# Row maxima of an attention round in one instruction instead of two, with other margins in the planner that lists the kernel's instructions

## The chip, the cores and the metric

The kernel runs on one core of a Trainium2 chip. The metric is the device time of one execution in microseconds (us); of several executions the median is given. Five engines work side by side, each through its own list of instructions in order: PE (TensorE, matrix products), DVE (VectorE), ACT (ScalarE), POOL (GpSimd) and SP (SyncE, which here only issues DMA transfers). Semaphores hold an instruction back until what it needs is there. PE writes to PSUM, a small memory of eight banks; everything else lies in SBUF or in the chip's main memory.

## The reference

The work is an attention over 8 batches and 8 heads of 576 tokens with 64 dimensions, which leaves out every score that is more than tau under the maximum of its row, and then an MLP mixer over tokens (576 to 256 to 576) and channels (512 to 1536 to 512). All is float32.

```python
scores = scale * np.matmul(q, k.transpose(0, 1, 3, 2))
thresh = np.max(scores, axis=-1, keepdims=True) - tau
scores = np.where(scores >= thresh, scores, -1000000000.0)
attn = np.exp(scores - np.max(scores, axis=-1, keepdims=True))
attn = attn / (np.sum(attn, axis=-1, keepdims=True) + 1e-09)
x = np.matmul(attn, v)          # then (B,H,S,D) -> (B, S, H*D)
h = np.maximum(x.transpose(0, 2, 1) @ w_tok1, 0.0) @ w_tok2
u = x + h.transpose(0, 2, 1)
out = u + np.maximum(u @ w_ch1, 0.0) @ w_ch2
```

## The kernel before, in words

**Tiles and stages.** Attention is cut into 144 units: 128 query rows (two heads of one batch side by side) against all 576 keys, 18 units to a batch. Two units make a round, 72 rounds in all, nine to a batch ("row" in the code). A round goes through all engines:

- PE forms the scores of both units and both heads (`scores_of_two`, line 1000) in the tile `sc`, which takes five of the eight banks. There is one such tile, so the next round's scores can't begin before the masks of this round have read it. The two heads lie at the two ends of the tile (`AT`, line 959): head 0 of both units in columns 0 to 1152, head 1 in columns 1408 to 2560. Both touch the third bank.
- DVE takes the maximum of each row (`top`, line 1025): one instruction for head 0 of both units and one for head 1, 1152 elements for each partition.
- POOL turns the maxima into the bias of the threshold (`shift`, line 1031), again one instruction for each head, of two elements for each partition.
- ACT applies the mask (`mask`, line 1043), four instructions of 576 elements, and the exponential with its sum (`exps`, line 1053), four more. Each of these is followed by a short read of the sum. The masks read `sc`; when all four are done, `sc` is free.
- DVE inverts the sums (lines 309 and 310), POOL scales the weights (`scale`, line 318), DVE transposes them in blocks (`T`, line 346), SP moves the blocks to their places (`eT`, line 356), and PE multiplies them with the values (line 404). In the first batch PE transposes instead (line 333, copied out in line 338) and the values are line 388.

The mixer's products are mixed in between: the token products of a batch (lines 485, 522, 535, 553) and its channel products (lines 1243, 1167, 1258). For each batch only a part of the channel products is done during attention. The rest is spilled to main memory and done after the last round, in a long stage of products by Strassen's scheme (line 1663). In the first 110 us the weights are also unpacked from a wide form on ACT, DVE and POOL (lines 228 to 252), and PE is given transposes that nobody reads (`keep_warm`, line 775) where it would stand still.

**Who sets the order.** When the program is built, a planner (`Scheduler`, lines 662 to 830) holds a clock for each engine and a list of operations with a cost in us, an engine, a rank and what they depend on. It always lists next the operation that can start first by its clocks, and of those that can start at once the one with the lower rank. The list is fixed from then on; on the chip each engine runs through its list and waits where something is late. What the planner counts therefore decides which work stands ahead of which, and nothing else. An operation may start at the end of what it depends on, plus that operation's `lag` (0.2 unless given) when it comes from another engine.

In a round (`make_round`, lines 1411 to 1465) the planner counts `SCORES` for the scores, 1.27 for each maximum, 0.24 for each shift, 0.64 for each mask with a lag of 0.25, 0.77 for each exponential. The loop over the masks goes over the heads outside and the units inside. A mask depends on the shift and the maximum of its head; those of the odd unit depend on the maximum of head 1 as well.

**The margins that the change touches.**

- `SLACK` and `SPARE` (line 636; `sure`, lines 698 to 702): an operation of PE that could start at once stands behind others if what it depends on ended less than `SLACK` ago on another engine, or landed less than `SPARE` ago.
- `NEAR`, `KEEP` and `KEEP_LAST` (lines 637, 730, 1059, 1496): scores are held until the mixer's products done so far reach a planned amount, less `KEEP` (for the last row `KEEP_LAST`), and less `NEAR` right behind values.
- `FLIGHT`, `RATE`, `LANDING` (lines 638, 707, 753 to 760): the planner's picture of the transfers: so many in flight at once, so many KB for each us, so long to land.
- `LATE` and `LATE_PE` (lines 705 and 706): once PE's clock is past `CALM`, an operation of DVE or PE that needs a transfer is planned this much after the landing.
- `WARM_GAP` and `WARM_TURN` (line 770): how many warm-up transposes are put into a gap of PE in the first 110 us.
- `SCORES` (line 1058): cost of a score block.

Of the kernel before, what the change touches and what calls it, by code (L numbers as in the profile page):

```python
# [14 lines left out]
ALU = mybir.AluOpType  # L15
AX = mybir.AxisListType
# [5 lines left out]
def kernel(  # L22
# [25 lines left out]
    nc = tc.nc  # L48
    B, H, S, D = q.shape
# [18 lines left out]
    SCALE = 1.0 / 8.0  # L68
# [192 lines left out]
    toff = const.tile([P, 1], F32, name="toff")  # L261
# [44 lines left out]
    def inverse(us):  # L306
        rs = sums_of[us[0] // 2 % RS]
        rr = small.tile([P, 2, 2], F32, tag="rr", name=f"rr_{us[0]}")
        nc.vector.tensor_reduce(out=rr, in_=rs, axis=AX.X, op=ALU.add)
        nc.vector.reciprocal(out=rr, in_=rr)  # L310
        for i, u in enumerate(us):
            st[u] = st[u][0], rr[:, i]

    def scale(u):
        e, rr = st[u]
        for h in range(2):
            eh = half(u, e, h)
            nc.gpsimd.tensor_scalar(out=eh, in0=eh, scalar1=rr[:, h : h + 1], scalar2=1.0, op0=ALU.mult, op1=ALU.mult)  # L318
        st[u] = e
# [23 lines left out]
    def turn_blocks(u):  # L343

        T = Ts[u] = att.tile([P, 4, NK * 32], F32, tag="T", bufs=3, name=f"T_{u}")
        nc.vector.transpose(out=T, in_=st.pop(u).rearrange("p a c x -> p a (c x)"))  # L346
# [286 lines left out]
        nc.vector.tensor_scalar(out=ntau, in0=toff, scalar1=SCALE, scalar2=None, op0=ALU.mult)  # L633

    TOKEN_RANK, TOKEN_AFTER_TOKEN = 1.5, 2.5
    SLACK, SPARE = 0.8, 3.5
    NEAR = 8
    FLIGHT, RATE, LANDING, LATE, LATE_PE, CALM = 12, 205.0, 1.5, 1.0, 0.0, 200.0
    WARM_UNTIL, WARM_GAP, WARM_TURN = 110.0, 0.6, 0.11

    class Op:

# [15 lines left out]
    class Scheduler:  # L658
# [59 lines left out]
        def pick(self, eng):  # L718
# [3 lines left out]
            for x in self.ready[eng]:  # L722
# [6 lines left out]
                c = t if t > now + 0.02 else now, eng == "pe" and self.sure(x) > now + 0.02, rank, x.index  # L729
                if x.rank == 1 and eng == "pe" and self.done < x.plan - (NEAR if self.after_values else 0.0):  # L730
                    held = c, t, x
# [109 lines left out]
    sched = Scheduler()  # L841
# [3 lines left out]
    def key_op(*key):  # L845
        return keyed.get(key)

    def put(key, x):
        keyed[key] = x
        return x  # L850
# [45 lines left out]
    def rank_of_group(b, p0, g):  # L896
        return ((b * NP + p0) // 2) * 3 + g
# [61 lines left out]
    AT = (0, 5 * MAIN - 2 * S)  # L959
# [60 lines left out]
            st[u] = [sc[:, at + S * k : at + S * k + S] for at in AT], bias[:, :, k : k + 1]  # L1020

    tops = {}
    def top(it, h):
        sc, mx, _ = tops[it]
        nc.vector.tensor_reduce(  # L1025
            out=mx[:, h], in_=sc[:, AT[h] : AT[h] + 2 * S].rearrange("p (k x) -> p k x", k=2), axis=AX.X, op=ALU.max
        )

    def shift(it, h):
        _, mx, bias = tops[it]  # L1030
        nc.gpsimd.tensor_scalar(out=bias[:, h], in0=mx[:, h], scalar1=toff, scalar2=-SCALE, op0=ALU.add, op1=ALU.mult)  # L1031

    def mask(u, h):
        if h == 0:
            part, bias = st[u]
            rs = sums_of[u // 2 % RS][:, u % 2]
            e = home_of(u)
            masked[u] = e, rs, part, bias
        e, rs, part, bias = masked[u]
        scores = part[h]  # L1040
        if in_blocks(units[u][0]):
            scores = scores.rearrange("p (a c y) -> p a c y", a=4, c=NK)
        nc.scalar.activation(out=half(u, e, h), in_=scores, func=AF.Prelu, bias=bias[:, h], scale=SCALE, alpha=STEEP)  # L1043
        if h == 1:
            del masked[u]
            st[u] = e, rs
# [3 lines left out]
    def exps(u, h):  # L1050
        e, rs = st[u] if u not in masked else masked[u][0:2]
        eh = half(u, e, h)
        nc.scalar.activation(out=eh, in_=eh, func=AF.Exp, bias=ntau, accum_out=rs[:, h, 0:1])  # L1053
# [1 line left out]

    UNITS = len(units)
    ROUNDS = UNITS // 2
    SCORES, VALUES, VALUES_IN_HALVES = 2.2, 3.45, 3.3
    KEEP, KEEP_LAST = 22.5, 25.5


    fills = {}
# [348 lines left out]
    def make_round(it):  # L1411
        us = (2 * it, 2 * it + 1)
        pre = [key_op("pre", u - 2, h) for u in us for h in range(2)]
        prepared = []
        for u in us:
            b, p0, t = units[u]
            n = b * NP + p0
            for m in [n] * (t <= SHARED) + [n + 1] * (t >= SHARED):
                prepared += [key_op("prep", m, 0) if it else None, key_op("prep", m, 1)]
                prepared += [key_op("prep", 0, "first")] if not it else []  # L1420
        x = put(("S", it), sched.op("pe", SCORES, lambda: scores_of_two(us, keyed["S", it].mark_eng), pre + prepared, 1 if it >= UB // 2 else -1))
        urgent = -1 if it < UB // 2 else 0
        row, k = divmod(it, UB // 2)
        x.plan = planned_at(row - 1, k) if row else -1.0
        x.scores = True
        for h in range(2):
            put(("mx", it, h), sched.op("dve", 1.27, lambda h=h: top(it, h), (x,), urgent))
            put(("bias", it, h), sched.op("pool", 0.24, lambda h=h: shift(it, h), (key_op("mx", it, h),), urgent))
        for h in range(2):
            for u in us:  # L1430
                deps = [key_op("bias", it, h), key_op("mx", it, h)]
                if h == 0:
                    deps += [key_op("T", u - 4), key_op("pre", u - 1, 0)]
                else:
                    deps.append(key_op("pre", u, 0))
                if u % 2:
                    deps.append(key_op("mx", it, 1))
                put(("pre", u, h), sched.op("act", 0.64, lambda u=u, h=h: mask(u, h), deps, urgent or 1, lag=0.25))
        for u in us:
            for h in range(2):  # L1440
                put(("exp", u, h), sched.op("act", 0.77, lambda u=u, h=h: exps(u, h), (key_op("pre", u, h),), 2, lag=0.3))
        n = sched.op("dve", 0.38, lambda: inverse(us), [key_op("exp", u, h) for u in us for h in range(2)], 2)
        for u in us:
            b, p0, t = units[u]
            s = sched.op("pool", 1.46, lambda u=u: scale(u), (n,), 1)
            deps = [s]
            G = rank_of_group(b, p0, t // GU)
            opens, closes = [u == end(where[b, p0, t - t % GU + i] for i in range(GU)) for end in (min, max)]
            if not b:
                deps += [key_op("V", G - 2) if opens else None, key_op("T", u - 1)]  # L1450
                for third in range(3):
                    x, y = sched.banked(
                        0.33,
                        lambda bank, u=u, third=third: turn(u, third, bank),
                        "act",
                        0.4,
                        lambda bank, u=u, third=third: turned(u, third, bank, nc.scalar.copy),
                        deps,
                        0,
                        other=("dve", 0.5, lambda bank, u=u, third=third: turned(u, third, bank, nc.vector.tensor_copy)),  # L1460
                    )
                    put(("turned", u, third), y)
                    deps = [x]
                put(("T", u), x)
                if closes:
                    make_group(b, p0, t // GU)
                    if t // GU == 2 and p0:
                        rows_due.append(b)
                continue
            deps += [key_op("T", u - 1), key_op("M", u - 3)]  # L1470
            put(("T", u), sched.op("dve", 1.31, lambda u=u: turn_blocks(u), deps, 4))
            put(
                ("M", u),
                sched.op(
                    "sp",
                    2.4,
                    lambda u=u: move(u),
                    (key_op("T", u), key_op("V", G - 2) if opens else None),
                    0,
                    after=(key_op("M", u - 1),),  # L1480
                    dmas=(4, 147, 0.69),
                ),
            )
            if closes:
                make_group(b, p0, t // GU)
                if t // GU == 2:
                    (rows_due if p0 == NP - 2 else early_due).append(b)
# [3 lines left out]
    def planned_at(row, k):  # L1491

        work = [TOKENS - SAVED * (r > 0) + NOW[r] * SEVEN + (GROUP - SEVEN) * (not r) for r in range(B - 1)] + [0.0]
        total = sum(work[:row])
        part = work[row]
        return total + part * (k - 2) / (UB // 2) - (KEEP_LAST if row == B - 2 else KEEP)
# [529 lines left out]
```

## Time and profile before

| what | us |
|---|---|
| median of 3 runs (1209.57 to 1210.18) | 1209.9 |
| the profiled execution | 1203.62 |
| its span, first to last instruction | 1201.8 |
| PE busy in 0 to 110 us / 110 to 793 / 793 to 1202 | 101.90 / 666.30 / 404.12 |
| of it warm-up transposes up to 110 us | 30.75 |
| DVE, ACT and POOL busy in the span | 881.9, 608.9, 336.6 |
| first and last maximum of a round start at | 8.6 and 789.2 |
| one maximum (1152 elements), one shift (2 elements) | 1.344, 0.276 |
| one mask, one exponential (576 elements) | 0.742, 0.784 |

The profile was taken by the hardware in one execution. An instruction's line in it is a line of the kernel. A group's row has its busy time, the mean duration of one in ns, and, behind the bar, how long the engine stood idle ahead of them and which engine's instruction ended that. A wait is put down to the instruction that came last. PE's busy time is modelled from the starts, so it is no measure of how close PE is to its peak. In the timeline a row has the start in us, the duration from the first to the last instruction of a merged group, the engine, the line, what is written and read, how many instructions it merges, and in brackets the idle time ahead.

### The profile page before, as it was taken

Reading aid. Unit: us, or ns where it says so; the run is one execution under the profiler, and the core shown is the slowest. Engines: PE = TensorE matmul, PEld = TensorE weight load, DVE = VectorE, ACT = ScalarE, POOL = GpSimd, SP = SyncE. Lnnn points to the kernel's source line nnn. Section 1 sums busy time; section 2 is a strip of 40 time slices with the busy share of each in tenths; the row PEclk is TensorE's granted clock in tenths of the full one; section 3 lists DMA queues with packets and bytes.
Section 4 is the critical chain, followed back from the end, with each engine's and each line's share of the span. In section 5 each row is a group of like instructions: output and inputs, shape, how many; then the busy total and the mean of one; then the engine's idle time right before and its main releaser. Section 6 shows DMA issues by size and latency. Waiting matters only on the chain.

```text
span 1201.8 us, 29350 instructions
## 1 busy us (share of the span) xinstructions
PE 1172.3 (98%) x11526; PEld 979.0 (81%) x11526; DVE 881.9 (73%) x1504; ACT 608.9 (51%) x1392; POOL 336.6 (28%) x577
## 2 busy tenths in 40 slices
PE   8999999999989999999999999999999999999998
PEld 7666878877768768877887887888899999999988
DVE  6788987678578668757866866854778687786866
ACT  6999775555664566555555556541231413223230
POOL 3576553244235324423433423421100000000000
PEclk9999999999999999999999999999999999999999
DMA  7655877678778778777877877671210302122020
GB/s 151 146 138 151 213 193 196 148 164 209 171 163 196 174 177 190 186 166 192 198 171 178 196 187 163 177 186 43 92 36 10 84 15 71 36 51 56 12 60 36
DMA packets 302154, 161.73 MB, mean 135 GB/s; under 512 B 191744, under 2 KB 287040, under 8 KB 301888
## 3 DMA queue, kind: packets, MB, share of 16 engines
q1 hardware_dynamic: 299856, 159.11, 54.9%
q8 instruction: 91, 1.49, 0.5%
q10 hardware_dynamic: 2160, 0.74, 0.2%
q14 instruction: 47, 0.39, 0.1%
HBM read 56.75 MB, written 14.68 MB: 59 GB/s over the span
## 4 chain that ended last, share of the span: by engine, by line
PE 69%; ACT 9%; DVE 7%; SPq 6%; DMA 5%; issue 2%; POOL 2%; DVEq 0%; ACTq 0%; POOLq 0%
PE bank L1663 29%; PE bank L1167 10%; PE bank L1243 8%; PE sc L1000 8%; PE bank L404 7%; ACT e L1043 4%; DVE mx L1025 4%; ACT e L1053 3%; SPq L356 3%; DMA eT<-T 2%; PE bank L553 2%; SPq L119 2%; PE bank L1258 2%; POOL e L318 2%; PE bank L522 1%
## 5 line engine op out<-in xcount | busy, mean ns | idle before, releaser
L1043 ACT ACTIVATE e<-sc,bias 128x576 f32<-128x576 f32 x288 | 194.3, 742 | 205.4 <-DVE mx L1025 102.0
L318 POOL TENSOR_SCALAR e<-e,rr 128x576 f32<-128x576 f32 x288 | 216.3, 771 | 128.9 <-DVE rr L310 106.5
L1053 ACT ACTIVATE e<-e,ntau 128x576 f32<-128x576 f32 x288 | 221.5, 784 | 0.6
L1025 DVE TENSOR_REDUCE mx<-sc 128x2 f32<-128x1152 f32 x144 | 187.6, 1344 | 34.7 <-PE sc L1000 34.6
L346 DVE STREAM_TRANSPOSE T<-e 128x1152 f32<-128x1152 f32 x126 | 170.0, 1360 | 16.9 <-POOL e L318 15.0
L1243 PE MATMUL bank<-xT,wc 128*128 128x256 f32 x768 | 175.1, 383 | 0.0
L1000 PE MATMUL sc<-kT,qT 64*64 64x384 f32 (+2 forms) x3456 | 159.6, 327 | 10.1 <-ACT e L1043 10.0
L1243 PEld LDWEIGHTS bank<-xT,wc 128*128 128x128 f32 x768 | 143.2, 190 | 25.1 <-issue 4.6
L1000 PEld LDWEIGHTS sc<-kT,qT 64*64 64x64 f32 x3456 | 101.3, 133 | 69.0 <-issue 46.2
L404 PE MATMUL bank<-eT,lv 64*64 64x192 f32 x3024 | 136.4, 325 | 7.8 <-DMA eT<-T 5.9
L404 PEld LDWEIGHTS bank<-eT,lv 64*64 64x64 f32 x3024 | 115.0, 133 | 26.9 <-issue 6.1
L1778 ACT COPY temps<-bank 128x256 f32<-128x256 f32 x90 | 33.4, 371 | 90.2 <-PE bank L1663 90.2
L1167 PE MATMUL bank<-wc,g 128*128 128x256 f32 x336 | 76.3, 379 | 0.0
L1167 PEld LDWEIGHTS bank<-wc,g 128*128 128x128 f32 x336 | 63.6, 190 | 8.7
L553 PE MATMUL bank<-w,a 128*128 128x192 f32 (+1 forms) x256 | 67.0, 412 | 0.0
L968 POOL MEMSET mark_pool<- 128x1 f32 x57 | 5.8, 103 | 207.3 <-PE sc L1000 178.9
L1031 POOL TENSOR_SCALAR bias<-mx,toff 128x2 f32<-128x2 f32 x144 | 39.2, 276 | 81.4 <-DVE mx L1025 79.2
L1663 PE MATMUL bank<-t,w1s 128*128 128x256 f32 x240 | 60.6, 379 | 0.0
L1167 PE MATMUL bank<-w2s,g 128*128 128x256 f32 x252 | 59.9, 387 | 0.7 <-DVE g L1131 0.7
L1053 ACT ACTIVATION_READ_ACCUMULATOR e<-e,ntau 128x1 f32 x288 | 59.9, 208 | 0.0
L1663 PE MATMUL bank<-t,wc 128*128 128x256 f32 x240 | 59.3, 379 | 0.0
L1663 PE MATMUL bank<-u,wc 128*128 128x256 f32 x240 | 58.5, 379 | 0.0
(196 smaller groups left out, 1834.2 us busy)
## 6 DMA issues: line engine op xcount, KB each, us to landing
eT<-T SPq DMA_DIRECT2D x504, 144.0 KB, 3.0
lv<-in_v_dram SPq DMA_DIRECT2D x112, 144.0 KB, 3.0
w2s<-in_moe_w_ch_dram SPq DMA_DIRECT2D x24, 512.0 KB, 3.9
lk<-in_k_dram SPq DMA_DIRECT2D x122, 72.0 KB, 3.0
ut<-us SPq DMA_DIRECT2D x136, 64.0 KB, 2.1
lq<-in_q_dram SPq DMA_DIRECT2D x120, 72.0 KB, 2.9
out_dram<-us SPq DMA_DIRECT2D x30, 256.0 KB, 2.7
u<-spill SPq DMA_DIRECT2D x8, 512.0 KB, 4.5
```

The lines of the kernel that those rows point to most:

```text
L318: nc.gpsimd.tensor_scalar(out=eh, in0=eh, scalar1=rr[:, h : h + 1], scalar2=1.0, op0=ALU.mult, op1=ALU.mult)
L346: nc.vector.transpose(out=T, in_=st.pop(u).rearrange("p a c x -> p a (c x)"))
L404: nc.tensor.matmul(to[o], lhsT=lv[half][r, c, :], rhs=eT[r, M * half : M * half + M, c, :], start=c == 0, stop=c == NK - 1, skip_group_che ...
L553: nc.tensor.matmul(bank[:, n * i : n * i + n], lhsT=hidden[b][:, m, P * c : P * c + P], rhs=w2[:, m, lo : lo + n], start=(m == 0), stop=(m ...
L1000: x = nc.tensor.matmul(sc[rows, at + lo : at + hi], lhsT=qT[r, cols], rhs=kT[r, lo:hi], start=True, stop=True, skip_group_check=True,)
L1025: nc.vector.tensor_reduce(out=mx[:, h], in_=sc[:, AT[h] : AT[h] + 2 * S].rearrange("p (k x) -> p k x", k=2), axis=AX.X, op=ALU.max)
L1031: nc.gpsimd.tensor_scalar(out=bias[:, h], in0=mx[:, h], scalar1=toff, scalar2=-SCALE, op0=ALU.add, op1=ALU.mult)
L1043: nc.scalar.activation(out=half(u, e, h), in_=scores, func=AF.Prelu, bias=bias[:, h], scale=SCALE, alpha=STEEP)
L1053: nc.scalar.activation(out=eh, in_=eh, func=AF.Exp, bias=ntau, accum_out=rs[:, h, 0:1])
L1167: nc.tensor.matmul(bank[:, 0:HD], lhsT=x[:, j, :], rhs=y[:, j, :], start=j == 0, stop=j == HJ - 1)
L1243: nc.tensor.matmul(bank[:, 0:n], lhsT=wc1[:, j, c, :], rhs=uT[:, c, GR * i : GR * i + n], start=(c == 0), stop=(c == NCC - 1))
L1663: nc.tensor.matmul(to, lhsT=l, rhs=r, start=start and x == 0, stop=x == len(pairs) - 1, skip_group_check=not start)
```

## The change

The two maxima of a round become one instruction that reads both ends of the score tile, and the two shifts become one. In the planner the round has one maximum of 2.53 us and one shift of 0.25, all four masks depend on these, and the odd unit's extra dependence goes. Ten of the planner's numbers change: `SLACK`, `SPARE`, `NEAR`, `FLIGHT`, `RATE`, `LATE_PE`, `WARM_GAP`, `SCORES`, `KEEP` and `KEEP_LAST`. What is computed stays the same.

```diff
@@ -633,10 +633,10 @@
         nc.vector.tensor_scalar(out=ntau, in0=toff, scalar1=SCALE, scalar2=None, op0=ALU.mult)
 
     TOKEN_RANK, TOKEN_AFTER_TOKEN = 1.5, 2.5
-    SLACK, SPARE = 0.8, 3.5
-    NEAR = 8
-    FLIGHT, RATE, LANDING, LATE, LATE_PE, CALM = 12, 205.0, 1.5, 1.0, 0.0, 200.0
-    WARM_UNTIL, WARM_GAP, WARM_TURN = 110.0, 0.6, 0.11
+    SLACK, SPARE = 1.0, 4.5
+    NEAR = 12.0
+    FLIGHT, RATE, LANDING, LATE, LATE_PE, CALM = 8, 214.0, 1.5, 1.0, 1.0, 200.0
+    WARM_UNTIL, WARM_GAP, WARM_TURN = 110.0, 0.4, 0.11
 
     class Op:
 
@@ -1020,15 +1020,14 @@
             st[u] = [sc[:, at + S * k : at + S * k + S] for at in AT], bias[:, :, k : k + 1]
 
     tops = {}
-    def top(it, h):
+    def top(it):
         sc, mx, _ = tops[it]
-        nc.vector.tensor_reduce(
-            out=mx[:, h], in_=sc[:, AT[h] : AT[h] + 2 * S].rearrange("p (k x) -> p k x", k=2), axis=AX.X, op=ALU.max
-        )
-
-    def shift(it, h):
+        both = bass.AP(tensor=sc.tensor, offset=sc.offset, ap=[sc.ap[0], [AT[1], 2], [S, 2], [1, S]])
+        nc.vector.tensor_reduce(out=mx, in_=both, axis=AX.X, op=ALU.max)
+
+    def shift(it):
         _, mx, bias = tops[it]
-        nc.gpsimd.tensor_scalar(out=bias[:, h], in0=mx[:, h], scalar1=toff, scalar2=-SCALE, op0=ALU.add, op1=ALU.mult)
+        nc.gpsimd.tensor_scalar(out=bias, in0=mx, scalar1=toff, scalar2=-SCALE, op0=ALU.add, op1=ALU.mult)
 
     def mask(u, h):
         if h == 0:
@@ -1055,8 +1054,8 @@
 
     UNITS = len(units)
     ROUNDS = UNITS // 2
-    SCORES, VALUES, VALUES_IN_HALVES = 2.2, 3.45, 3.3
-    KEEP, KEEP_LAST = 22.5, 25.5
+    SCORES, VALUES, VALUES_IN_HALVES = 2.4, 3.45, 3.3
+    KEEP, KEEP_LAST = 26.0, 27.0
 
 
     fills = {}
@@ -1423,18 +1422,15 @@
         row, k = divmod(it, UB // 2)
         x.plan = planned_at(row - 1, k) if row else -1.0
         x.scores = True
-        for h in range(2):
-            put(("mx", it, h), sched.op("dve", 1.27, lambda h=h: top(it, h), (x,), urgent))
-            put(("bias", it, h), sched.op("pool", 0.24, lambda h=h: shift(it, h), (key_op("mx", it, h),), urgent))
+        put(("mx", it), sched.op("dve", 2.53, lambda: top(it), (x,), urgent))
+        put(("bias", it), sched.op("pool", 0.25, lambda: shift(it), (key_op("mx", it),), urgent))
         for h in range(2):
             for u in us:
-                deps = [key_op("bias", it, h), key_op("mx", it, h)]
+                deps = [key_op("bias", it), key_op("mx", it)]
                 if h == 0:
                     deps += [key_op("T", u - 4), key_op("pre", u - 1, 0)]
                 else:
                     deps.append(key_op("pre", u, 0))
-                if u % 2:
-                    deps.append(key_op("mx", it, 1))
                 put(("pre", u, h), sched.op("act", 0.64, lambda u=u, h=h: mask(u, h), deps, urgent or 1, lag=0.25))
         for u in us:
             for h in range(2):
```

## The prediction

> **What bounds the kernel now.** I read the page first, then busy time by stage, then the waits of PE between 160 and 793 us, then the timeline of single rounds.
>
> ```profile
> PE 1172.3 (98%) x11526; PEld 979.0 (81%) x11526; DVE 881.9 (73%) x1504; ACT 608.9 (51%) x1392; POOL 336.6 (28%) x577
> PE 69%; ACT 9%; DVE 7%; SPq 6%; DMA 5%; issue 2%; POOL 2%; DVEq 0%; ACTq 0%; POOLq 0%
> 0.00:110.00 110.00, 101.90 (x1118) 76.74 (x1118) 85.43 (x154) 93.80 (x197) 63.42 (x105) 1.00 0.63 143
> 110.00:793.00 683.00, 666.30 (x7773) 531.84 (x7774) 504.51 (x690) 405.40 (x894) 262.73 (x463) 1.00 0.77 183
> 793.00:1202.00 409.00, 404.12 (x2637) 370.44 (x2635) 291.99 (x662) 109.72 (x303) 10.44 (x9) 1.00 0.18 52
> ```
>
> PE is busy for 98% of the span at clock 1.00, and the chain that ended last is 69% PE. So an edit off PE counts only where PE waits for it. There are three stages (columns: PE, PEld, DVE, ACT, POOL). Up to 110 us, 30.75 us of PE's busy time are warm-up transposes on a scratch bank (line 775), which are no work: there the time is set by the chain of a round and by ACT, 93.80 of 110 us busy. From 110 to 793 us PE has attention and channel products to mix and idles for 16.7 us. After 793 us no rounds are left, and I cost the change at nothing there (PE busy for 404 of 409 us).
>
> ```profile
> PE sc L1000 <- ACT e L1043: 6.3, 3, 2.6
> PE bank L404 <- DMA eT<-T: 5.9, 3, 2.8
> PE bank L404 <- DVE qT L288: 1.0, 1, 1.0
> ```
>
> These are PE's waits from 160 to 793 us (total, times, longest): three for the masks that free the score tile, three for a moved block of weights. The rest of PE's idle time there is in pieces under 1 us. So about 13 us are there to be won in the middle. One of the three score waits in the timeline:
>
> ```profile
> 520.24 2.58 DVE L1025 TENSOR_REDUCE mx<-sc 128x2 f32<-128x1152 f32 x2
> ...
> 521.65 0.27 POOL L1031 TENSOR_SCALAR bias<-mx,toff 128x2 f32<-128x2 f32 x1 [2.89 <-DVE mx L1025]
> 522.74 0.40 DVE L1251 TENSOR_SCALAR g<-bank 128x256 f32<-128x256 f32 x1
> 522.91 0.27 POOL L1031 TENSOR_SCALAR bias<-mx,toff 128x2 f32<-128x2 f32 x1 [1.00 <-DVE mx L1025]
> 522.91 0.74 ACT L1043 ACTIVATE e<-sc,bias 128x576 f32<-128x576 f32 x1 [2.87 <-DVE mx L1025]
> ...
> 524.46 1.98 ACT L1043 ACTIVATE e<-sc,bias 128x576 f32<-128x576 f32 x3
> ...
> 526.49 0.77 PE L1000 MATMUL sc<-kT,qT 64*64 64x128 f32 x12 [2.06 <-ACT e L1043]
> ```
>
> The first shift is done at 521.92, but the first mask starts at 522.91, 0.09 us after the *second* maximum ended (522.82). I went through all 72 rounds: the first mask never starts less than 0.09 us after the second maximum, in 51 of them within 0.2 us, and in most of the others one shift of POOL behind a scaling (line 318) ended last. So today's split gains the masks nothing: they already run behind both maxima.
>
> **The change, part by part.** *Maximum.* Two reductions become one of 2304 elements.
>
> ```profile
> L1025 DVE TENSOR_REDUCE mx<-sc 128x2 f32<-128x1152 f32 x144 | 187.6, 1344 | 34.7 <-PE sc L1000 34.6
> L309 DVE TENSOR_REDUCE rr<-rs 128x4 f32<-128x8 f32 x72 | 10.9, 152 | 61.1 <-ACT e L1053 61.0
> L1031 POOL TENSOR_SCALAR bias<-mx,toff 128x2 f32<-128x2 f32 x144 | 39.2, 276 | 81.4 <-DVE mx L1025 79.2
> ```
>
> From the first two rows an element costs (1344 - 152)/(1152 - 8) = 1.042 ns. One of 2304 takes 1344 + 1152 x 1.042 = 2.55 us, an estimate; the ends are 2.40 (no fixed part) and 2.69 (two full ones). I take 2.55, by the line through both rows. Back to back the two take 2.62 now (median from the first's start to the second's end), so the pair is 0.07 shorter, 72 x 0.07 = 5 us of DVE. DVE is 73% busy and PE covers that: worth nothing by itself.
>
> *Shift.* One of 4 elements for two of 2: between nothing and 0.55 us, and I take one row, 0.28, because the width hardly counts at so few elements. It takes 72 x 0.28 = 20 us off POOL, 28% busy: nothing. But it now lies between the maximum and the first mask. A shift ends 0.36 us after the maximum it needs where POOL is free (46 of the 72 second ones), and a mask follows a shift by 0.03. From the end of the scores to the first mask: now 0.07 + 2.62 + 0.12 = 2.81 us; then 0.07 + 2.55 + 0.36 + 0.03 = 3.01. So **+0.20 us per round** (ends: +0.05 and +0.61). Where a scaling holds POOL, the shift waits as long as today: nothing.
>
> Whom does this hit? 19 score blocks start within 0.2 us of the last mask before them; nine of these start by 117.2 us, where no other work of PE covers them, and ten later, where the order decides (below). 9 x 0.20 = **+1.8 us** (0.5 to 5.5).
>
> The Trainium skill (Perfetto Trace Analysis, Optimizing Scalar/DVE Operations) puts VectorE's overhead per instruction on PSUM at about 125 ns, where the rows give 0.07 us. By it the added latency would be 0.14, and the nine rounds 1.3 us instead of 1.8.
>
> *The list.* The order on every engine is written by the planner, so its costs matter more than the instruction. Before: the planner lets the first mask start 0.2 + 1.27 + 0.2 + 0.24 + 0.2 = 2.11 us after the scores, the odd unit's at 2.94 (its tie to the second maximum), the fourth ends at 4.86, and with 0.25 of lag and 2.2 for the scores a round closes on itself in 7.31 us. The chip's shortest rounds take 7.66 and 7.69: the plan is 0.37 short. After: 0.2 + 2.53 + 0.2 + 0.25 + 0.2 = 3.38, plus 4 x 0.64 and 0.25 is 6.19, plus 2.4 is 8.59; the chip would need 7.68 + 0.20 = 7.88. The plan is now 0.7 long, 1.28 longer than before. Where a score block had nothing ahead of it but the masks, about 1.28 us more of other PE work is listed ahead. The three score waits past 160 us (6.3 us) should shrink by 3 x 1.28 = **-3.8 us**.
>
> LATE_PE goes from 0 to 1.0: past 200 us PE's work behind a landing is planned 1 us later, and other work is drawn ahead. Of the three waits for eT (5.9 us) that takes 3 x 1.0 = **-3.0 us** (0 to -5.9). SLACK and SPARE choose surer work of equal start, the same way, with no number of their own. FLIGHT 8: a move is four transfers at 0.69 us with some 2.2 us from issue to landing in the plan, three or four in flight, so it binds only among the loads of the start; RATE 214: 147 KB take 0.69 us, as long as the issue. Both are nothing, with a bound of 1.5 us either way at the start. WARM_GAP 0.4 adds two warm transposes ahead of a score block; they end 0.4 us ahead of a time that is planned late: nothing. NEAR and the KEEPs let score blocks go about 3.5 us of channel work earlier; the fill is the same in sum. No transfer, copy or product is added or taken away; moved ones come out of the list.
>
> Sum: 1.8 - 3.8 - 3.0 = -5.0 us. The profiled execution took 1203.62 us (span 1201.8), 0.5% under the median of the runs shown, 1209.9; there it would be 1198.6, and in the runs 1209.9 x 1198.6/1203.6 = **1204.9**.
>
> **The rivals.** *Slower: the start pays.* Up to 110 us PE has only warm-up to hide a round, and ACT is busy for 93.80 us, in order. With the masks planned 1.27 us later, the planner fits one more ACT instruction ahead of them (a conversion of 0.69, an exponential of 0.78 and 0.21); where the scores come on time it holds the masks, and with them the next scores. Price: 11 score blocks after the first up to 117 us x (0.20 + 0.70) = 9.9 us, which nothing later gives back, since PE is full from there: 1209.9 + 9.9 = 1219.8, or 1216.4 if half of the 6.8 us of the middle is won. It decides once the score block that starts at 106.4 us now starts more than 6.8 us later. For it: the chain there has no cover. Against: ACT still idles for 16 us there, and a plan nearer to the chip's order should cost less, not more.
>
> *A wash.* The 1.28 us that a score block is put back comes out again at its values (line 404), which wait one step later in the same chain; then only +1.8 is left of the sum, 1211.7, or 1208.3 with half of the 6.8. For it: the waits for eT show that the values have no reserve either. Against: PE idles in few places, and most rounds have 1 to 4 us between the last mask and the next scores.
>
> *The split was worth its time.* If the first mask did use the early half, joining would cost 1.27 us in each of the 19 tight rounds, 24 us: 1234. The 72 rounds speak against it, none has an early mask. The Trainium skill (same page and section) says that where VectorE isn't saturated but makes other engines wait, breaking instructions up may let work finish sooner. That is this rival; by it 1234, and the trace disagrees, with the 0.09 us above.
>
> **How the numbers follow.** Forecast 0.48 (1194 to 1207), slower start 0.29 (1212 to 1220), wash 0.20 (1206 to 1213), the split's worth 0.03. A measurement tells 0.2% (2.4 us) from no change. Of the wash, 0.04 lie under 1207.5, 0.10 within 0.2% and 0.06 above. Faster 0.48 + 0.04 = 0.52, same 0.10, slower 0.29 + 0.06 + 0.03 = 0.38. The range reaches from all of PE's 16.7 idle us of the middle won at the lower end of the start's cost (1209.9 + 0.5 - 16.7 = 1193.7) to the slower start in full (1219.8): 1194 to 1220. It leaves out only the split's worth and the ends of the cases, under 0.2.
>
> **What would show it.** One reduction of 2.5 to 2.6 us and one shift per round, the first mask 0.4 us after the maximum; the score block of 106.4 us within 2 us of that; PE's waits for masks past 160 us under 3 us and for eT under 3 us. I am wrong if the start is longer by over 5 us, if the values' waits grow by what the scores' lose, or if the reduction takes over 2.7 us.

## The result, and the profile after

The changed kernel takes 1215.87 us (median of 16 runs, 1209.56 to 1222.19); the kernel before took 1209.74 beside it (16 runs, 1202.13 to 1215.74). The ratio is **1.0048**, 95% interval 1.0031 to 1.0065: slower by 5.8 us. Two later measurements of the same kernel gave 1.0027 and 1.0035. The forecast was 1204.9 us and faster. The time lies inside the range of 1194 to 1220, but on the other side of no change.

The changed kernel's profiled execution took 1211.73 us, its span 1209.9. The page, busy time and the chain of waits:

```profile
PE 1176.6 (97%) x11530; PEld 982.1 (81%) x11530; DVE 880.2 (73%) x1432; ACT 608.6 (50%) x1395; POOL 321.6 (27%) x502
...
PE 70%; SPq 7%; DMA 7%; ACT 6%; DVE 5%; issue 3%; POOL 2%; DVEq 0%; ACTq 0%; POOLq 0%
```

Busy time by stage (columns as before), cut where the last round now ends, at 802 us:

```profile
0.00:110.00 110.00, 100.53 (x1106) 76.21 (x1110) 83.28 (x139) 94.52 (x201) 61.48 (x99) 1.00 0.66 148
110.00:802.00 692.00, 673.35 (x7802) 537.25 (x7795) 505.15 (x634) 406.99 (x899) 249.73 (x395) 1.00 0.76 180
802.00:1210.00 408.00, 402.70 (x2628) 368.65 (x2626) 291.77 (x660) 107.05 (x298) 10.43 (x9) 1.00 0.18 51
```

Nothing has moved from one engine to another. The last stage is the same (5.3 us without PE, 4.9 before). The middle is 9 us longer: 2 us of that are idle time of PE (18.65 us instead of 16.7). The other 7 are PE's busy time, partly because a stage that begins at 110 us does not begin at the same work, partly because some products ran slower. A table further down compares the traces where the same products are done.

The joined instruction, its mean, and the masks behind it (groups of the page):

```profile
L1042 ACT ACTIVATE e<-sc,bias 128x576 f32<-128x576 f32 x288 | 194.4, 744 | 171.1 <-POOL bias L1030 171.1
...
L1026 DVE TENSOR_REDUCE mx<-sc 128x4 f32<-128x2304 f32 x72 | 183.1, 2544 | 39.1 <-PE sc L1000 38.8
```

One reduction takes 2.544 us (2.55 predicted). Where POOL is free, a shift ends 0.36 us after the maximum and the first mask starts 0.03 later; 0.4 was predicted. PE's waits from 160 to 802 us (total, times, longest):

```profile
PE bank L404 <- DMA eT<-T: 6.1, 5, 2.2
PE sc L1000 <- ACT e L1042: 4.8, 1, 4.8
PE bank L404 <- DMA lv<-in_v_dram: 1.9, 1, 1.9
PE sc L1000 <- DVE qT L288: 1.4, 1, 1.4
PE bank L404 <- ACT g L1247: 1.1, 3, 0.5
PE bank L535 <- DMA x_sb<-x_sb: 0.9, 2, 0.5
```

The three score waits for masks (6.3 us) have become one, but it is 4.8 us long, and waits for `qT`, `lv` and `g` stand beside it. In the timeline of the changed kernel around that one wait, the number in brackets is the idle time ahead:

```profile
327.56 2.14 PE L1000 MATMUL sc<-kT,qT 64*64 64x128 f32 x48
...
329.63 1.09 PE L485 MATMUL bank<-ident,xT 128*128 128x128 f32 x8
329.94 2.52 DVE L1026 TENSOR_REDUCE mx<-sc 128x4 f32<-128x2304 f32 x1
...
332.55 0.27 POOL L1030 TENSOR_SCALAR bias<-mx,toff 128x4 f32<-128x4 f32 x1 [2.51 <-DVE mx L1026]
332.85 2.64 ACT L1042 ACTIVATE e<-sc,bias 128x576 f32<-128x576 f32 x4 [1.45 <-POOL bias L1030]
...
335.54 4.12 PE L1000 MATMUL sc<-kT,qT 64*64 64x128 f32 x48 [4.82 <-ACT e L1042]
...
339.44 3.58 PE L404 MATMUL bank<-eT,lv 64*64 64x192 f32 x72
```

Between the scores of rounds 29 and 30 PE has only eight transposes, 1.09 us of work, where the round takes 7.98 (327.56 to 335.54). It stands still until the fourth mask is done, and then the same 48 matmuls take 4.12 us instead of 2.14. The record of the granted clock shows half speed for 6.827 us from 333.57. The kernel before has 13.1 us from scores to scores at this place, all but 0.9 us of it work:

```profile
326.56 2.14 PE L1000 MATMUL sc<-kT,qT 64*64 64x128 f32 x48
328.63 1.31 PE L485 MATMUL bank<-ident,xT 128*128 128x128 f32 x10
329.96 7.17 PE L522 MATMUL bank<-x_sb,w 128*128 128x256 f32 x32
337.06 0.70 PE L535 MATMUL bank<-x_sb,w 64*128 64x256 f32 x2
338.63 1.13 PE L535 MATMUL bank<-x_sb,w 64*128 64x256 f32 x6 [0.87 <-DMA x_sb<-x_sb]
339.69 2.19 PE L1000 MATMUL sc<-kT,qT 64*64 64x128 f32 x48
```

Ten transposes, not eight: the last two (0.4 us) turn the last 64 tokens, and the token products (line 522, 7.17 us) need them. In the changed kernel they come only at 342.94, and the products at 343.47.

Why the planner left them out can be followed while it builds the list. At its own time of 332.37 these two transposes are ready and have a bank. But a step that short (`x.short`) is set aside unless a score block can start right behind it, and is taken up again only if nothing else is ready. In the changed plan the values of line 404 are already known to be ready at 338.27 and the scores at 337.74. So something else is there, 5.4 us later, and the step is not taken up:

```python
if x.short and self.early and not any(y.scores and self.start(y, eng) <= t + x.cost + 0.1 for y in self.ready[eng]):
    aside = c, t, x
    continue
...
if best is None:
    best = aside
```

The stop is thus in the list itself: it is planned at 5.37 us. The longest stop that the plan of before has past 112 us is 1.64. With the rule on short steps left out, the planner's list for the changed kernel has no stop there, and none over 2.23 us past 112 us; that list was not timed.

One trace is a thin measure here. The same kernel's executions lie 1% apart, and the first profiled execution of before (span 1201.8) was one of its shortest; a second had a span of 1209.8. So the verdicts below rest on the ratios, and the traces show where things happen.

### The profile page after: what moved, and what is told of

The parts are those of the page before. It is cut to its first block, busy times and chain, and to the rows that moved or that the text cites. A ratio compares the mean times of both kernels' runs of the same rounds, so it can differ in the third digit from the quotient of the medians.

```text
span 1209.9 us, 29141 instructions
## 1 busy us (share of the span) xinstructions
PE 1176.6 (97%) x11530; PEld 982.1 (81%) x11530; DVE 880.2 (73%) x1432; ACT 608.6 (50%) x1395; POOL 321.6 (27%) x502
## 4 chain that ended last, share of the span: by engine, by line
PE 70%; SPq 7%; DMA 7%; ACT 6%; DVE 5%; issue 3%; POOL 2%; DVEq 0%; ACTq 0%; POOLq 0%
PE bank L1659 29%; PE bank L1166 10%; PE bank L1242 9%; PE bank L404 8%; PE sc L1000 7%; SPq L356 4%; PE bank L553 3%; SPq L119 2%; DMA w2s<-in_moe_w_ch_dram 2%; ACT e L1052 2%; ACT e L1042 2%; PE bank L522 2%; DVE mx L1026 2%; PE bank L1257 1%; DMA eT<-T 1%
## 5 line engine op out<-in xcount | busy, mean ns | idle before, releaser
L1026 DVE TENSOR_REDUCE mx<-sc 128x4 f32<-128x2304 f32 x72 | 183.1, 2544 | 39.1 <-PE sc L1000 38.8
L1000 PE MATMUL sc<-kT,qT 64*64 64x384 f32 (+2 forms) x3456 | 162.5, 330 | 9.1 <-ACT e L1042 7.4
L1000 PEld LDWEIGHTS sc<-kT,qT 64*64 64x64 f32 x3456 | 104.6, 135 | 67.8 <-issue 45.9
L1166 PE MATMUL bank<-w2s,g 128*128 128x256 f32 x252 | 59.6, 386 | 1.2 <-DVE g L1130 1.2
L1052 ACT ACTIVATION_READ_ACCUMULATOR e<-e,ntau 128x1 f32 x288 | 59.9, 208 | 0.0
L1247 ACT ACTIVATE g<-bank 128x256 f32<-128x256 f32 x64 | 24.8, 388 | 69.5 <-PE bank L1242 69.3
```

Source lines behind the costliest of these rows:

```text
L1000: x = nc.tensor.matmul(sc[rows, at + lo : at + hi], lhsT=qT[r, cols], rhs=kT[r, lo:hi], start=True, stop=True, skip_group_check=True,)
L1026: nc.vector.tensor_reduce(out=mx, in_=both, axis=AX.X, op=ALU.max)
L1166: nc.tensor.matmul(bank[:, 0:HD], lhsT=x[:, j, :], rhs=y[:, j, :], start=j == 0, stop=j == HJ - 1)
```

## The experiments

**Which half of the change?** Theory A: the new order costs the time, and the joined instruction costs little. Theory B, its rival: the joined instruction's latency costs it. The first kernel joins the instructions and keeps the list of before, row by row; the second keeps the changed list and splits the instructions.

```diff
 def top(it, h):                 # first kernel; shift alike
+    if h: return
-    nc.vector.tensor_reduce(out=mx[:, h], in_=<head h>, ...)
+    nc.vector.tensor_reduce(out=mx, in_=<both heads>, ...)
```

> The joined maximum and the joined shift, listed where the first of the two stood before; every other engine's list is that of the kernel before, row by row. Theory A (the loss of the change is in the list: one score block listed where PE has nothing else, 4.8 us of waiting and 6.8 us at half clock behind it): within 2.5 us of the kernel before, -1 to +2.5, no wait of PE for masks over 3 us. Theory B (the joined instruction itself, +0.2 us and more in every tight round): 4 to 6 us slower than before, as the whole change.

> The list of the changed kernel, with the two maxima and two shifts of before in the place of the joined ones. Theory A: as slow as the changed kernel, 4 to 8 us over before, with the wait of PE of 4 to 5 us for the masks near 330 us and the half clock behind it. Theory B: back to the kernel before, within 2 us.

Measured: 1.0018 (1.0003 to 1.0033) for the first and, timed again beside others, 1.0010 (0.9993 to 1.0028); 1.0053 (1.0038 to 1.0069) for the second, with the stop again (4.57 us, half clock for 6.83). So the joined instruction costs about 0.14% (the mean of the two), 1.7 us. The three measurements of the changed kernel have a mean of 1.0037; the other 0.23%, 2.8 us, is in the list, and splitting the instructions again does not give it back. B falls.

**The round's costs or the margins?** Here A1 holds the longer planned round for the cause and A2 the margins. The third kernel has the changed round in the planner with all ten old numbers, the fourth the old round with the new numbers.

```diff
-SLACK, SPARE = 1.0, 4.5         # third kernel: these and the other eight as before
+SLACK, SPARE = 0.8, 3.5
```

> The joined instructions with the planner's new costs for the round (2.53 and 0.25, all masks behind both), all ten margins as before. Theory A1 (the longer planned round makes the bad place): slower than before by 4 to 10 us, a wait of PE over 4 us for masks. Theory A2 (the margins make it): within 3 us of before, no wait over 3 us. Theory B: 4 to 6 us slower without such a wait.

> Maxima, shifts and their planned costs as before, the ten margins of the change. Theory A1: within 3 us of before. Theory A2: 4 to 10 us slower, with a wait of PE over 4 us and time at half clock. Theory B: as before, within 2 us.

Measured: 1.0312 (1.0292 to 1.0332) and 1.0537 (1.0515 to 1.0559). Each half alone is six to eleven times worse than both. PE's waits from 160 to 802 us of the third and of the fourth:

```profile
PE sc L1000 <- ACT e L1042: 13.9, 5, 5.7
PE bank L404 <- issue: 7.5, 4, 2.6
PE bank L404 <- DMA eT<-T: 7.4, 6, 2.2
```

```profile
PE bank L404 <- DMA eT<-T: 23.1, 7, 7.5
PE bank L404 <- DMA lv<-in_v_dram: 7.6, 1, 7.6
PE sc L1000 <- ACT e L1043: 7.5, 3, 3.0
```

These are other lists, not the old one with something added. Neither half has a price of its own, and both expectations fell with that. (`NEAR` and the two `KEEP`s turned out to do nothing: with their old values the changed list comes out the same, row by row.)

**Is it the stop, or its clock?** Theory C: the halved clock behind the stop costs 2.5 to 4 us. The fifth kernel puts 36 transposes that nobody reads into the stop.

```diff
-if eng == "pe" and t < WARM_UNTIL:
-    self.keep_warm(t)
+if eng == "pe" and (t < WARM_UNTIL or x.scores and t - self.clock["pe"] > 4.0):
+    self.keep_warm(t if t < WARM_UNTIL else t - 1.0)
```

> The changed kernel, row by row, with 36 transposes that nobody reads put into the one stop that its own list plans (the scores behind the thirtieth round's, near 330 us); nothing else moves. Theory C (the stop costs twice: 4.8 us of standing still, and then 6.8 us at half clock because PE was idle through a window of the clock's gate, which is 3.4 us): the half clock at 333 us is gone, the score block takes 2.2 us instead of 4.1, and the time is 2.5 to 4 us under the changed kernel's, ratio to before 1.002 to 1.003. Theory D (the half clock has nothing to do with idling, or the time is lost anyway further on): no change against 1.0048.

Measured: 1.0030 (1.0016 to 1.0045), clock 1.0 throughout. That lies between the first two measurements of the changed kernel (1.0048 and 1.0027), so both were timed again on one chip, with the split put back in the filled list as well:

> The changed kernel itself, timed beside the three that follow on one chip, so that their ratios share the runs of before. Theory G (the loss is the joined instruction, 0.18%, plus one stop with its halved clock, some 0.25%): 1.0040. Theory H (the loss lies in the list as a whole, in scattered waits for moved blocks, and not in the stop): 1.003 to 1.005 too. This run only sets the level.

> The changed kernel with 36 transposes that nobody reads in its planned stop, so that the clock is not halved. Theory G: 0.25% under the changed kernel timed beside it, 1.0015 to 1.0020. Theory H: within 0.1% of it, 1.003 or above.

> The changed list with two maxima and two shifts in place of the joined ones, and with the stop filled by the same transposes. Theory G: nothing of the loss is left, 0.999 to 1.001. Theory H: 1.003 or above, since the list is still the changed one.

> The joined instructions in the list of before, row by row, once more beside the others. Theory G: 1.0018, as the stop is not in this list. Theory H: 1.0015 to 1.002 too; if H holds, this and the filled changed kernel differ by over 0.1%, under G they are equal.

Measured: changed kernel 1.0035 (1.0014 to 1.0056), filled 1.0034 (1.0014 to 1.0053), filled and split 1.0065 (1.0040 to 1.0089), joined in the old list 1.0010. The filled kernel's two measurements have a mean of 1.0032, the changed kernel's three 1.0037: filling is worth 0.05%, less than these intervals can tell from nothing and less than C and G ask for. The timeline of the second filled trace shows what can become of it:

```profile
330.91 4.09 PE L775 MATMUL warm<-ident 128*128 128x128 f32 x36
335.89 2.19 PE L1000 MATMUL sc<-kT,qT 64*64 64x128 f32 x48 [0.89 <-ACT e L1042]
339.56 0.54 PE L404 MATMUL bank<-eT,lv 64*64 64x192 f32 x4 [1.48 <-DMA eT<-T]
```

The scores run at full clock again, but the values behind them now wait 1.48 us for their block. From the scores' start to the values' start it is 3.67 us here and 3.90 in the changed kernel, so here the next wait had hidden the slow clock. In the first filled trace that wait was 0.61 us and the time 2.80; even so, five score blocks on, neither of the two is ahead of the changed kernel by more than 1 us (the table below). The fill is not work, so the stop itself remained. In this list the split is no better (1.0065 against 1.0034), which refutes G a second time.

**Do the small waits count?** The seventh kernel is before with unread transposes ahead of its waits of 1.7 to 2.9 us, so that the clock stays up.

```diff
+elif eng == "pe" and x.scores and x.number in {15: 16, 38: 10, 47: 13}:
+    ...  # so many transposes ahead of the scores; 9 more inside the values of batches 3 to 7
```

> The kernel before with transposes that nobody reads in seven places where its profile shows PE waiting 1.4 to 3 us (three score blocks, the second group of values of batches 3 to 7), each shorter than the wait. Theory C: no wait is shortened, but fewer windows at half clock, so 1 to 5 us faster than before and a narrower spread of the runs. Theory D: 0 to 2 us slower, by the transposes where nothing waits.

Measured: 0.9999 (0.9982 to 1.0017). The mean granted clock of its twelve executions is 0.9991, and 0.9966 in the 29 of before beside it. So the transposes did keep the clock up for the most part, and the time stayed the same to within 0.2%. Over 124 executions of before, the slower ones do tend to have the lower clock (correlation -0.59; -1 would be a straight line). With this run, that is better read as waits that make both than as drops that make the time.

**Other numbers in the planner.** Lists with no planned stop over 1.8 us, found by trying margins in the plan alone:

```diff
+SLACK .8, RATE 205                                          # sixth kernel
+SLACK .9, SPARE 5, FLIGHT 12, RATE 205, LATE .5, LATE_PE 1.5, SCORES 2.3,
+    maximum 2.55, shift .27                                   # eighth
+SLACK .7, SPARE 5, FLIGHT 8, RATE 210, LATE_PE .5           # ninth: round and instructions split, as before
+SLACK .75, FLIGHT 12, RATE 200, LATE_PE 0, SCORES 2.1, maximum counted at 1.9   # tenth
```

> The changed kernel with two margins that matter set otherwise (SLACK 0.8 for 1.0, RATE 205 for 214; NEAR and the KEEPs too, which leave the list as it is), so that the planner's list has no stop of PE over 1.3 us past 110 us, where the changed kernel's has one of 5.4. Theory A (the loss is that stop and its clock): 3 to 6 us under the changed kernel, ratio to before 0.998 to 1.002. Theory B (the joined instruction costs in every round): stays at 1.004 to 1.006.

> The joined maximum and shift with a third set of margins (SLACK 0.9, SPARE 5, FLIGHT 12, RATE 205, LATE 0.5, LATE_PE 1.5, SCORES 2.3, planned costs 2.55 and 0.27), whose list has no planned stop over 1.8 us past 110 us. Theory A: ratio to before 0.995 to 1.002. Theory B: 1.004 or more, as the changed kernel.

> Maxima, shifts and their planned costs as before (two and two), with other margins (SLACK 0.7, SPARE 5, FLIGHT 8, RATE 210, LATE_PE 0.5) whose list has no planned stop of PE over 1.3 us past 110 us and no more planned idling than that of before. Theory E (what matters is only that the margins before are a well fitted list, and any other gapless list is some 0.3 to 0.5% behind it, joined or not): ratio to before 1.003 to 1.006. Theory F (the planned length of the joined round makes the lists worse; a gapless list of the short round is as good as before): 0.998 to 1.002.

> The joined instructions, with the maximum planned too short (1.9 us, it takes 2.55) and margins SLACK 0.75, SPARE 4.5, FLIGHT 12, RATE 200, LATE_PE 0, SCORES 2.1, whose list has no planned stop over 1.7 us past 110 us. Theory F: a short plan packs the rounds closer, ratio to before 0.996 to 1.002. Theory E: 1.003 to 1.006 like the others.

Measured: 1.0048 (1.0032 to 1.0064), 1.0033 (1.0013 to 1.0054), 1.0118 (1.0097 to 1.0139) and 0.9993 (0.9979 to 1.0008). The ninth, slower than any expectation had it, shows that the numbers of before are a good fit and not any fit; the tenth that the joined instruction is no worse than the split one in a list fitted to it. It plans the maximum 0.6 us short of its true time. No planned stop is thus not enough: these four plan nearly the same idle time for PE between 112 and 800 us (8.4 to 9.3 us) and lie 1.2% apart.

**Second looks.** Two more traces, of before and of the changed kernel:

> The kernel before once more, for a second trace: the first one was an execution 0.5% under the median. Every theory expects the same list and the same waits in the same places, with spans from 1202 to 1212 us; it shows how much of the first trace's distance to the changed kernel (8.1 us) is that execution's luck.

> The changed kernel once more, for a second trace and on the chip of these runs. Theory C: the stop of 4.5 to 5 us near 330 us and the half clock behind it again, in each execution. Ratio to before 1.003 to 1.0065.

Measured: spans of 1209.8 and 1212.2, the latter timed at 1.0027 (1.0012 to 1.0043). The stop is there again (4.80 us, half clock for 6.83). With these, four traces of the old list and three of the changed one can be compared by the waits of PE in three stretches (sums of the views' rows, us):

| list (traces) | 115 to 305 | 305 to 350 | 350 to 800 | of these for masks |
|---|---|---|---|---|
| before, split (2) | 3.6, 3.6 | 0.9, 0.5 | 11.1, 13.7 | 3.7, 4.4 |
| before, joined (2) | 4.6, 4.5 | 0.4, 0.2 | 12.7, 11.2 | 6.0, 3.3 |
| changed (3) | 3.2, 2.1, 3.2 | 4.8, 4.8, 5.0 | 10.0, 12.4, 9.8 | 0, 0, 0 |

The longer plan did take away the waits for masks behind 350 us, all of them. Beside those for `eT` now stand waits for `lv` (1.3 to 2.8 us, once a trace), `g` (1.1 to 1.3), `T` (2.2 and 2.3 in two of the three) and, as before, `qT` and `x_sb`. One wait was traded for another, and the stop at 330 us came on top.

**The two ends of the list.** The last two kernels have joined instructions throughout and change the planner's numbers on the way: changed up to 305 us and old behind, and old up to 370 us and changed behind.

```diff
+PLANS = NEW, OLD                # the other kernel: OLD, NEW
+TURN, TURN_ROUND = 305.0, 27    # the other kernel: 370.0, 33
+def __getitem__(self, name):
+    return PLANS[self.clock["pe"] >= TURN][name]
```

> Joined instructions throughout. The changed margins and round costs up to round 27 (PE's planned clock at 305 us), those of before from there on. The list is the changed one up to there, but has no planned stop at 332 us (longest planned stop 1.18 us). Theory S (the planned stop itself, with PE out of work, is the loss, and filling it with transposes could not give it back): 0.998 to 1.001. Theory H (the changed list loses in other places too): 1.003 or above if these lie ahead of 305 us.

> Joined instructions throughout. The margins and round costs of before up to round 33 (PE's planned clock at 370 us), the changed ones from there on. No planned stop over 1.64 us. Theory S: the level of the joined instructions in the list of before, 1.000 to 1.002. Theory H: 1.003 or above if the changed list's losses lie behind 370 us.

Measured: **0.9983** (0.9967 to 0.9999) and **1.0054** (1.0036 to 1.0072). Neither has the stop. From 300 to 350 us the first has the two transposes in their place:

```profile
326.15 2.14 PE L1008 MATMUL sc<-kT,qT 64*64 64x128 f32 x48
328.23 1.31 PE L485 MATMUL bank<-ident,xT 128*128 128x128 f32 x10
329.56 7.17 PE L522 MATMUL bank<-x_sb,w 128*128 128x256 f32 x32
```

In the first kernel PE's list is the changed one up to about 315 us of the trace and that of before from about 415 us on. In the second it stays that of before up to about 415 us, though the numbers change earlier, and is the changed one from there on. So the halves can be priced against the joined instruction in the old list (1.0014). The changed early half, without its stop, is worth -0.31% (about 0.20 either way, from both intervals). The changed late half costs +0.40% (about 0.22). Together with 1.0014 they make 1.0023; the changed kernel has 1.0037, so 0.14% or 1.7 us is left for the changed list between 315 and 415 us, the stop among it, which these intervals can't tell from nothing.

The traces say more about that stretch. Score block k opens round k, counted from 0. Ahead of block 29 (the one before the stop), of block 34 and of block 38, PE has done the same products in every list of the table, in other orders, but for transposes that nobody reads. Block 34 starts here, in the first traces of before and of the changed kernel:

```profile
381.87 2.14 PE L1000 MATMUL sc<-kT,qT 64*64 64x128 f32 x48
```

```profile
386.28 2.19 PE L1000 MATMUL sc<-kT,qT 64*64 64x128 f32 x48
```

The times from start to start can thus be compared (us):

| list (traces) | block 29 starts at | 29 to 34 | 34 to 38 | 38 to the end |
|---|---|---|---|---|
| before, split (2) | 326.6, 327.9 | 55.3, 56.2 | 46.1, 45.8 | 773.8, 779.9 |
| before with filled waits, split (1) | 326.7 | 53.7 | 45.7 | 781.7 |
| before, joined (2) | 329.4, 330.6 | 53.8, 54.0 | 46.2, 45.7 | 777.3, 778.1 |
| changed (3) | 327.6, 326.6, 326.4 | 58.7, 59.5, 59.5 | 44.4, 44.4, 44.4 | 779.3, 781.7, 780.3 |
| changed, filled (2) | 325.9, 327.9 | 58.5, 59.6 | 44.4, 44.4 | 779.7, 780.1 |
| changed, split, without and with the fill (2) | 327.4, 326.7 | 59.9, 58.1 | 44.4, 44.4 | 784.5, 782.6 |
| changed until 305 (1) | 326.2 | 53.8 | 44.4 | 780.7 |
| old until 370 (1) | 328.0 | 54.2 | 46.7 | 783.0 |

From block 29 to 34 the seven traces with the stop take 58.1 to 59.9 us, the seven without it 53.7 to 56.2. The stop's 4.8 us are not made good among these five blocks, filled or not. Against the joined instruction in the old list the changed kernel gains 3.1 us ahead of block 29 (some 1.4 of it a half clock near 165 us in both of those traces, see the last section), loses 5.3 from there to block 34, gains 1.5 up to block 38, and is 2.7 longer behind it, where traces of one list lie up to 6 us apart. That makes 3.4 us in the span, where the timed runs have 2.8. Theory S, that the stop is all of the loss, has the first kernel right and falls with the second; H holds, for the late half. PE's waits from 350 to 800 us in the second kernel:

```profile
PE bank L404 <- DMA eT<-T: 9.4, 5, 2.8
PE sc L1008 <- DVE qT L288: 3.5, 2, 2.1
PE bank L404 <- ACT g L1254: 1.3, 3, 0.5
```

That makes 14.4 us with the small rows, where the changed kernel had 9.8 to 12.4, from about 415 us on with the same list of PE: the waits of this list spread widely from one execution to the next.

## Why the prediction was wrong, step by step

- **The joined instruction**, +1.8 us: right in size, and in mechanism as far as the instruction goes. The reduction took 2.544 us (2.55), the mask came 0.39 to 0.40 us after the maximum (0.39), score block 10, the one of 106.4 us, started at 108.3 (within 2 us), and in the old list the whole cost 0.14%, 1.7 us. That it arises in the nine rounds up to 117 us is not shown: block 10 starts at 107.5 and 108.0 us with the joined instruction in the old list, and at 106.4 and 108.2 in the two traces of before. The shift, 0.301 us in the mean, is a little longer than the row of two elements that I took (0.28).
- **"The three score waits past 160 us (6.3 us) should shrink by 3 x 1.28"**, -3.8 us, with **"moved ones come out of the list"**: the step that failed. Behind 350 us these waits went entirely (3.7 us to none), so the link from a longer plan to more work ahead of the scores holds. But I took the waits alone from a list that I left otherwise as it was. The new list put a stop of 4.8 us at 330 us, by the rule on short steps, which made the stretch from block 29 to 34 some 5 us longer, and other waits in the place of those that went. Waits from 350 to 800 us: 11.1 to 13.7 before, 9.8 to 12.4 after. In the sum the list was to give 6.8 us (3.8 and 3.0); in the timed runs it cost 2.8.
- **LATE_PE, -3.0 us** on the waits for `eT`: not borne out. Past 160 us they went from 5.9 us in three to 6.1 in five in the first traces. In the others they are 7.3 before, 3.6 and 6.7 with the joined instruction in the old list, 4.8 and 4.7 in the changed kernel: at best a part of the 3.0, inside the spread. `LATE_PE` was not changed alone in any run, but the fourth kernel speaks against adding up such effects: with the new numbers and the old round, `eT` alone costs 23.1 us.
- **"NEAR and the KEEPs let score blocks go about 3.5 us of channel work earlier"**: wrong, they leave the list as it is; at nothing in the sum this cost nothing.
- **Start and tail**: right. With the same products done, block 29 starts at 326.4 to 327.6 us, before at 326.6 and 327.9. Behind 802 us PE idles for 5.3 us (4.9).
- **The rivals.** *The start pays* is refuted: it decided from 6.8 us at the block of 106.4, which starts at 107.3 to 108.3 in the three traces of the changed kernel. *The split was worth its time* is refuted by the first and tenth kernels. The rule of the Trainium skill (Perfetto Trace Analysis, Optimizing Scalar/DVE Operations), that breaking instructions up may let work finish sooner, gains nothing here: in the changed list, splitting again made nothing faster, 1.0053 and 1.0065. *A wash* comes nearest: the waits moved on, to blocks, copies and loads. Its 1208.3 to 1211.7 was too low, for it knew no cost of the new order itself.

What stays open: whether and why the changed late half costs 0.4%. It shows in the timed runs of the last kernel; in the three traces of the changed kernel its waits come to no more than those of the old one, and from block 38 on they take 779.3 to 781.7 us, where the six traces of the old late list take 773.8 to 781.7. Only the trace of the last kernel has more of both (14.4 and 783.0). A profiled execution can lie some us under the median of its kernel (1211.7 against 1215.9 here, 1208.5 against 1212.2 for the joined instruction in the old list), so a few traces don't settle it. The planner's rule that made the stop was not altered in any timed run.

## What to carry to other kernels

Where a program lists its instructions by a planner, a cost or a margin is not a term in a sum: changing one refits the whole order, and here each half of a change that moved the time by 0.4% moved it by 3 and 5% alone. Predict the instruction from the profile, but for the order build the list and look for places where an engine is out of work; ask of every rule that sets work aside whether something far in the future can keep it there. Where orders differ, compare traces between points at which the same work is done: sums of waits hid what the stop cost, and the time from block to block shows it. The best list here joined the instructions and took the old numbers from 305 us on, 0.17% under before (0.01 to 0.33); as the best of ten lists, part of that may be luck.

## What the runs showed of the hardware

Within the span, PE's granted clock drops to half for 3.413 us or a multiple (6.827 behind the stop), at points on a grid of that step: within one execution they lie whole multiples of 3.413 us apart. A wait of 2.09 us (619.20 to 621.29 us, in the last kernel) had a drop at its end, at 621.15, while waits of 2.57 and 2.84 us in the first trace of before had none: it depends on where in the grid the wait falls. Cut by that grid, the 20 traces have, from 15 to 1195 us, 35 steps at full clock in which PE has no product running for over 2.0 us, and each is followed by a drop; no drop follows a step with under 1.4 us; between these bounds both occur. The Trainium skill (TensorE: Matmul & The Clock Gate, HAM oscillation — how this bites in real kernels) gives "no PE-idle gaps >~3.4µs" as the rule. The traces agree with the window of 3413 ns that the same page of the Trainium skill states (What's actually happening), but a wait of less than two thirds of that can be enough.

The halved clock need cost nothing: behind the stop it doubled a score block, 2 us, yet kept at full clock the filled kernel took as long from block 29 to 34. Elsewhere it can cost: near 165 us, behind a wait of 2.7 to 2.9 us, two traces of the joined instruction in the old list have a drop and take 23.0 and 22.9 us from block 14 to 16; the last kernel, with the same list there, a wait of 2.9 us and no drop, takes 21.5.
